# First feed-forward layer by seven products over halves, in units interleaved with the second layer

## The chip, the cores and the metric

The kernel runs on one core of a Trainium2 chip. The metric is the device time of one execution in microseconds (us), the median of several runs. Every run also records the span from its first to its last instruction and the mean clock that the throttle granted TensorE (1.000 is full speed). Runs over 1.5% above the fastest of the same kernel are marked slow and left out of the ratios. Each kernel was timed in rounds with the kernel before on the same chip.

## The reference

Linformer attention over 8 batches of 1024 tokens (8 heads of 64), then a feed-forward pair with a sigmoid-approximated gelu. Only the last two lines matter here.

```python
k_proj = einsum('ks,bhsd->bhkd', E, k);  v_proj = einsum('ks,bhsd->bhkd', F, v)
attn   = softmax(q @ k_proj.T / sqrt(64))          # 64 keys per head
x      = (attn @ v_proj) laid out as 8192 tokens x 512
h      = x @ w_in                                  # 512 -> 2048: the first layer
g      = h * sigmoid(1.702 * h)
out    = g @ w_out                                 # 2048 -> 512: the second layer
```

## The kernel before

The 8192 tokens are worked off in 16 blocks of 512. In each block, TensorE makes the first layer, then the second; scores, softmax sums and values of later blocks are slipped in between as short bursts. The second layer already takes seven products over halves in place of eight (Winograd's variant of Strassen's method): of g, of w_out and of the result each dimension is halved, sums of the halves are made beforehand, and products share banks of PSUM, in which they go on adding.

The first layer in plain form, 16 feature tiles x 4 matmuls of 512 columns, each tile in the next free bank, and read by ScalarE's gelu:

```python
def ffn1(j, fc, ts=slice(0, TB)):
    h_ps = f_tile([P, n])                          # 5 banks in turn
    for kc in range(KC):                           # 4
        nc.tensor.matmul(h_ps, w_in_sb[:, kc, fc*P:(fc+1)*P], xT[j][:, kc, ts], ...)
    nc.scalar.activation(gts[j][:, fc, ts], h_ps, AF.Gelu_apprx_sigmoid)
```

The sums of g for the second layer, on VectorE, made for 4, then 3, then 1 pairs of feature tiles as the gelus come in:

```python
def g_sums(j, c0, n):
    lo, hi = slice(c0, c0+n), slice(FH+c0, FH+c0+n)
    tt(t[0], g[:, lo, THI], g[:, hi, THI], op=ALU.add)       # for product 5
    tt(t[1], t[0], g[:, lo, TLO], op=ALU.subtract)           # for product 6
    tt(t[2], g[:, lo, TLO], g[:, lo, THI], op=ALU.subtract)  # for product 7
    tt(t[3], g[:, hi, TLO], t[1], op=ALU.subtract)           # for product 3
```

The second layer's parts, each of two halves of 8 matmuls with 256 columns. Products 1 and 2 add in one bank, 6, 7 and 4 in a second (which starts as a copy of product 1), 5 and 3 in a third:

```python
def prod(i, tc_, first, final):
    for k in range(FH):                            # 8
        nc.tensor.matmul(gb[bank[i]][:, tc_], a[:, k, tc_*P:(tc_+1)*P], w[:, k], ...)
...
return [p1a, p1b, p5a, p5b, h(6,0), p6b, h(2,0), p2b, h(7,0), p7b, h(4,0), p4b, h(3,0), p3b]
```

The softmax here doesn't subtract the row's maximum and nothing guards it: scores larger than these inputs give would overflow.

Of the kernel before, what the change touches and what calls it, by code (L numbers as in the profile page):

```python
# [17 lines left out]
def kernel(ctx, tc, q, k, v, E, F,  # L18
# [21 lines left out]
    ps_f = ctx.enter_context(tc.tile_pool(name="ps_f", bufs=4, space=PSUM))  # L40
    ps_g = ctx.enter_context(tc.tile_pool(name="ps_g", bufs=1, space=PSUM))
# [4 lines left out]
    ef_f = work.tile([P, JB, DM], F32, name="o_sb")[:, :S // DM].rearrange("p j m -> p (j m)")  # L46
    ef_sb = consts.tile([P, S], BF16, name="ef_sb")
# [84 lines left out]
    opening, f_next, g_next = [True], [0], [0]  # L132

    def f_tile(shape, dt=F32):
        if not opening[0]:
            f_next[0] += 1
            if f_next[0] % 5 == 0:
                return ps_g.tile(shape, dt, name="g3_ps")
        return ps_f.tile(shape, dt, name="f_ps")

    def x_any(shape, dt=F32):
        if not opening[0]:
            return f_tile(shape, dt)
        g_next[0] += 1
        return ps_g.tile(shape, dt, name=f"g{g_next[0] % 4}_ps")
# [18 lines left out]
    ffs = consts.tile([P, J, 2, KP], BF16, name="ffs")  # L164
# [69 lines left out]
    q0s = [[consts.tile([P, 2, 2, P], BF16, name=f"q0T{g}{u}") for u in range(2)] for g in range(2)]  # L234
# [65 lines left out]
    def sums(h):  # L300


        def go():
            d_ps = [x_any([P, TB]), ps_g.tile([P, TB], F32, name="g0_ps")]
            for p in range(HP):
                for e in range(2):
                    r = HI if (p + e) % 2 else LO
                    nc.tensor.matmul(d_ps[e][32 * p:32 * p + 32], ones[r, :32], expT[h][r, p, :], start=True, stop=True)
            den = att.tile([P, 2, TB], F32, name="den", bufs=1)
            for e in range(2):  # L310
                nc.vector.tensor_copy(den[:, e, :], d_ps[e])
            rdens[h] = den
        return go
# [59 lines left out]
    def tok0(p, a):  # L373
# [5 lines left out]
        if p not in xs:  # L379
            xs[p] = work.tile([P, 2, 2, 2, D], BF16, name="x0_sb", bufs=4)  # L380
# [35 lines left out]
    def ffn1(j, fc, ts=slice(0, TB)):  # L416
        if j not in gts:
            gts[j] = work.tile([P, FC, TB], BF16, name="gT", bufs=1)
# [7 lines left out]
    def ffn2(j, n, fcs):  # L426
        b, c = divmod(j, NB2)
        ov = out[b * S:(b + 1) * S, :].rearrange("(p j) m -> p j m", j=J)
        if j not in osb:
            osb[j] = work.tile([P, JB, DM], F32, name="o_sb")  # L430
# [5 lines left out]
        if fcs.stop == FC:  # L436
            nc.scalar.copy(osb[j][:, n, :], o_ps.pop(n))
            if n == JB - 1:
                nc.sync.dma_start(out=ov[:, c * JB:(c + 1) * JB, :], in_=osb[j])
# [7 lines left out]
    tw = consts.tile([P, 4, FH, MH], BF16, name="tw")  # L447
    sg = consts.tile([P, 4, FH, TH], BF16, name="sg")

    def w_sums():  # L450
# [3 lines left out]
        def tt(out_, in0, in1, op=ALU.subtract):  # L454
            def go():
                if not tmp:
                    tmp.append(work.tile([P, JB, DM], F32, name="o_sb").rearrange("p c (d m) -> p (c d) m", m=MH))
# [4 lines left out]
        return [tt(tw[:, 0], b12, b11), tt(None, b22, b12), tt(tw[:, 2], b22, b12), tt(None, None, b11, ALU.add),  # L462
                tt(tw[:, 3], b21, None), lambda: nc.vector.tensor_copy(tw[:, 1], tmp[0])]

    def g_sums(j, c0, n):
# [4 lines left out]
        tt(t[0], g[:, lo, THI], g[:, hi, THI], op=ALU.add)  # L470
        tt(t[1], t[0], g[:, lo, TLO], op=ALU.subtract)  # L471
        tt(t[2], g[:, lo, TLO], g[:, lo, THI], op=ALU.subtract)  # L472
        tt(t[3], g[:, hi, TLO], t[1], op=ALU.subtract)  # L473

    def ffn2_parts(j, last=False):



        b, c = divmod(j, NB2)
        ov = out[b * S:(b + 1) * S, :].rearrange("(p j) m -> p j m", j=J)[:, c * JB:(c + 1) * JB]  # L480
        o = osb[j] = work.tile([P, JB, DM], F32, name="o_sb")
# [5 lines left out]
        bank = {1: 0, 2: 0, 6: 1, 7: 1, 4: 1, 5: 2, 3: 2}  # L487
        gb, u, gl = {}, {}, []

        def prod(i, tc_, first, final):  # L490
            a, w = ops[i]
            for k in range(FH):
                nc.tensor.matmul(gb[bank[i]][:, tc_], a[:, k, tc_ * P:(tc_ + 1) * P], w[:, k],  # L493
                                 start=(first and tc_ == 0 and k == 0), stop=(final and k == FH - 1),
                                 skip_group_check=True)

        def tile_of(n):
            gb[n] = ps_g.tile([P, 2, MH], F32, name=f"g{n}_ps")

        def p1a():  # L500
            tile_of(0)
            prod(1, 0, True, False)

        def p1b():
            prod(1, 1, True, False)
            tile_of(1)
            nc.scalar.copy(gb[1], gb[0])

        def p5a():
            tile_of(2)  # L510
            prod(5, 0, True, False)

        def keep(n):
            u[n] = work.tile([P, 2, MH], F32, name=f"u{n}_sb", bufs=1)
            nc.scalar.copy(u[n], gb[n])  # L515

        def p5b():
            prod(5, 1, True, False)
            keep(2)

        def p6b():
            prod(6, 1, False, False)
            keep(1)

        def put(ts, ms):
            if last:
                nc.sync.dma_start(out=ov[:, ts, ms], in_=o[:, ts, ms])

        def p2b():
            prod(2, 1, False, True)  # L530
            nc.scalar.copy(o[:, 0:2, :MH], gb[0])  # L531
            put(slice(0, 2), slice(0, MH))

        def p7b():
            prod(7, 1, False, False)
            nc.vector.tensor_tensor(o[:, 2:4, MH:], gb[1], u[2], op=ALU.add)  # L536
            put(slice(2, 4), slice(MH, DM))

        def p4b():
            prod(4, 1, False, True)  # L540
            nc.scalar.copy(o[:, 2:4, :MH], gb[1])  # L541
            put(slice(2, 4), slice(0, MH))

        def p3b():
            prod(3, 1, False, True)
            nc.vector.tensor_tensor(o[:, 0:2, MH:], gb[2], u[1], op=ALU.add)
            nc.sync.dma_start(out=ov, in_=o)

        def p3l(tc_):
            def go():  # L550
                for k in range(FH):
                    nc.tensor.matmul(gl[tc_][:, :MH], sg[:, 3, k, tc_ * P:(tc_ + 1) * P], b22[:, k],
                                     start=False, stop=(k == FH - 1), skip_group_check=True)
                nc.vector.tensor_tensor(o[:, tc_, MH:], gl[tc_][:, :MH], u[1][:, tc_], op=ALU.add)
                put(slice(tc_, tc_ + 1), slice(MH, DM))
            return go

        def p5l(tc_):
            def go():
                gl.append(f_tile([P, TB]))  # L560
                for k in range(FH):
                    nc.tensor.matmul(gl[tc_][:, :MH], sg[:, 0, k, tc_ * P:(tc_ + 1) * P], tw[:, 0, k],
                                     start=(k == 0), stop=False, skip_group_check=True)
                if tc_ == 0:
                    u[2] = work.tile([P, 2, MH], F32, name="u2_sb", bufs=1)
                nc.scalar.copy(u[2][:, tc_], gl[tc_][:, :MH])
            return go

        h = lambda i, tc_: lambda: prod(i, tc_, False, False)
        if last:  # L570
            return [p1a, p1b, p5l(0), p5l(1), h(6, 0), p6b, h(2, 0), h(7, 0), p7b, p2b, h(4, 0), p4b, p3l(0), p3l(1)]
        return [p1a, p1b, p5a, p5b, h(6, 0), p6b, h(2, 0), p2b, h(7, 0), p7b,
                h(4, 0), p4b, h(3, 0), p3b]

# [46 lines left out]
    for i, f in enumerate(w_sums()):  # L621
# [19 lines left out]
    at(2, O + 1, scores(4, 0), values(3, 0))  # L641
    at(2, O + 6, scores(4, 1), values(3, 1))
    at(2, O + 9, scores(5, 0), sums(4), gather(4))
    at(2, O + 11, gelu_table)
    at(3, 2, q_dma(3))
    at(3, 3, proj(3), kv_out(3))
    for j in range(3, NBLK - 1):
        at(j, 1, spread(j + 1))
    for b in range(4, B):
        at(NB2 * b - 4, 2, q_dma(b))  # L650
    for j in range(3, NBLK - 1):
        if j + 2 < NBLK:
            at(j, O + 1, scores(j + 2, 1))
        at(j, O + 1, values(j + 1, 0))
        if j + 3 < NBLK:
            at(j, O + 9, scores(j + 3, 0))
        at(j, O + 9, values(j + 1, 1))
        if j + 2 < NBLK:
            at(j, O + 9, sums(j + 2), gather(j + 2))
            at(j, O + 11, gelu_table)  # L660
        if j % NB2 == 0 and j // NB2 + 2 < B:
            at(j, O + 9, proj(j // NB2 + 2), kv_out(j // NB2 + 2))

# [5 lines left out]
    for j in range(NBLK):  # L669
# [15 lines left out]
        if j == 1:  # L685
            opening[0] = False
            g1_ps = ps_g.tile([P, TB], F32, name="g1_ps")
            nc.tensor.matmul(g1_ps, zeros[:, :P], zeros, start=True, stop=True)
        for s, part in enumerate(ffn2_parts(j, j == NBLK - 1)):
            part()  # L690
            filled(j, O + s)
    assert not fill, fill
# [30 lines left out]
```

## Time and profile before

| | kernel before |
|---|---|
| time (three runs; a fourth came with the result) | 491.07 us (490.88 to 491.67) |
| span of the profiled run, granted clock | 489.6 us, 1.000 |
| TensorE, VectorE, ScalarE busy | 98%, 41%, 56% |
| one block without / with a k/v projection | 27.7 / 29.8 us |

The lines themselves stand in the prediction below, with what each column is. An entry in brackets at the end of a timeline line is the time that the engine had idled and what ended it. "PE" are matmuls, "PEld" the weight loads beside them; L numbers are lines of the kernel and differ between the two kernels (first layer: L422 before, L634 after; second layer: L493 before, L552 after).

### The profile page before, as it was taken

The page shows a single profiled execution, that of the slowest core. Times are in us where ns is not written, and L with a number is a line of the kernel's source. Part 1 is how long each engine was busy: PE and PEld are TensorE (multiplying, and loading weights), DVE is VectorE, ACT ScalarE, POOL GpSimd, SP SyncE. Part 2 cuts the span into 40 slices and gives each one's busy share as a digit, 9 for nine tenths or more (in the row PEclk, how much of TensorE's full clock was granted, in tenths as well). Part 3 has the DMA queues.
Part 4 walks back from the last instruction along what each step waited for, and adds up shares of the span by engine and source line. Part 5 has one row for each costly group of instructions (what it writes and reads, how often), then busy time and mean ns, then how long its engine had stood idle before and what let it go on. Part 6 is the DMA issues. An engine that isn't in the chain of part 4 may idle for free.

```text
span 489.6 us, 8708 instructions
## 1 busy us (share of the span) xinstructions
PE 478.1 (98%) x3672; PEld 297.8 (61%) x3707; DVE 202.0 (41%) x435; ACT 275.7 (56%) x445; POOL 83.0 (17%) x103
## 2 busy tenths in 40 slices
PE   8999999999999999999999999999999999999997
PEld 4645458466474755757575674757557474756656
DVE  4514786243542434444233543433453342335241
ACT  2665365465556557564665736575565656555361
POOL 7562251151070070006000240000000000000000
PEclk9999999999999999999999999999999999999999
DMA  9999999999899999699972999356240506032202
GB/s 169 200 189 207 223 160 167 207 212 215 174 94 219 170 183 217 151 172 114 211 143 103 170 113 246 71 171 90 95 87 26 149 1 174 4 124 52 87 0 87
DMA packets 131195, 69.09 MB, mean 141 GB/s; under 512 B 98116, under 2 KB 122708, under 8 KB 129236
## 3 DMA queue, kind: packets, MB, share of 16 engines
q0 software_dynamic: 86816, 30.43, 55.5%
q1 hardware_dynamic: 44260, 37.84, 31.2%
q8 instruction: 29, 0.48, 0.4%
q10 hardware_dynamic: 80, 0.26, 0.2%
q14 instruction: 10, 0.08, 0.1%
HBM read 72.88 MB, written 16.99 MB: 184 GB/s over the span
## 4 chain that ended last, share of the span: by engine, by line
PE 87%; DMA 7%; issue 2%; DVE 2%; ACT 1%; POOL 0%; DVEq 0%; POOLq 0%; ACTq 0%
PE f_ps L422 35%; PE g_ps L493 33%; PE g_ps L422 8%; DMA q_even<-in_q_dram 3%; PE f_ps L434 3%; DMA v_sb<-in_v_dram 3%; PE f_ps L181 2%; PE f_ps L270 2%; DVE o_sb L536 1%; DMA o_sb<-in_E_dram 1%; PE f_ps L189 1%; ACT o_sb L531 1%; ACT expT L289 1%; PE g_ps L150 1%; PE g_ps L270 1%
## 5 line engine op out<-in xcount | busy, mean ns | idle before, releaser
L422 PE MATMUL f_ps<-xT,w_in_sb 128*128 128x512 bf16 (+1 forms) x830 | 190.9, 377 | 1.4
L422 PEld LDWEIGHTS <-w_in_sb 128*128 128x128 bf16 x1032 | 100.6, 98 | 117.0 <-issue 1.2
L424 ACT ACTIVATE gT<-f_ps 128x512 bf16<-128x512 f32 (+1 forms) x214 | 126.9, 593 | 70.0 <-PE f_ps L422 69.0
L493 PEld LDWEIGHTS <-sg 128*128 128x128 bf16 x928 | 89.5, 98 | 16.0 <-DVE sg L473 5.2
L493 PE MATMUL g_ps<-tw,sg 128*128 128x256 bf16 x704 | 82.1, 273 | 0.0
L493 PEld LDWEIGHTS <-gT 128*128 128x128 bf16 x720 | 69.8, 98 | 18.4 <-issue 6.9
L470 DVE TENSOR_TENSOR sg<-gT 128x1024 bf16<-128x1024 bf16 (+2 forms) x45 | 22.9, 510 | 112.1 <-ACT gT L424 112.1
L69 POOL DMA_DIRECT2D q_sb<-in_q_dram x48 | 42.0, 904 | 158.8 <-DMA qT<-q_sb 134.8
L493 PE MATMUL g_ps<-w_out_sb,gT 128*128 128x256 bf16 x480 | 57.6, 273 | 0.0
L422 PE MATMUL g_ps<-xT,w_in_sb 128*128 128x512 bf16 x172 | 44.6, 379 | 0.2
L289 ACT ACTIVATE expT<-f_ps 128x512 bf16<-128x512 f32 (+1 forms) x50 | 26.7, 580 | 16.7 <-PE f_ps L270 13.5
L536 DVE TENSOR_TENSOR o_sb<-g_ps,u_sb 128x512 f32<-128x512 f32 x15 | 10.4, 691 | 62.1 <-PE g_ps L493 37.3
L354 DVE TENSOR_TENSOR xT<-f_ps,rbc 128x512 bf16<-128x512 f32 x40 | 26.2, 684 | 20.3 <-DMA rbc<-rdr 14.1
L424 ACT ACTIVATE gT<-g_ps 128x512 bf16<-128x512 f32 x44 | 26.3, 597 | 12.2 <-PE g_ps L422 11.6
L493 PE MATMUL g_ps<-tw,gT 128*128 128x256 bf16 x240 | 28.7, 272 | 1.5 <-DVE o_sb L536 1.1
L493 PE MATMUL g_ps<-w_out_sb,sg 128*128 128x256 bf16 x224 | 26.7, 273 | 0.0
L541 ACT COPY o_sb<-g_ps 128x512 f32<-128x512 f32 x15 | 8.8, 585 | 31.9 <-PE g_ps L493 31.9
L515 ACT COPY u_sb<-g_ps 128x512 f32<-128x512 f32 x29 | 17.1, 590 | 12.6 <-ACT u_sb L515 8.1
L471 DVE TENSOR_TENSOR sg<-sg,gT 128x1024 bf16<-128x1024 bf16 (+2 forms) x45 | 23.1, 514 | 1.6
L472 DVE TENSOR_TENSOR sg<-gT 128x1024 bf16<-128x1024 bf16 (+2 forms) x45 | 22.8, 507 | 0.0
L473 DVE TENSOR_TENSOR sg<-gT,sg 128x1024 bf16<-128x1024 bf16 (+2 forms) x45 | 22.8, 506 | 0.0
L293 ACT ACT_TABLE_LOAD x15 | 19.2, 1283 | 0.3
(120 smaller groups left out, 343.8 us busy)
## 6 DMA issues: line engine op xcount, KB each, us to landing
out_dram<-o_sb SPq DMA_DIRECT2D x15, 1024.0 KB, 3.9
rbc<-rdr SPq DMA_DIRECT2D x24, 512.0 KB, 5.3
k_sb<-in_k_dram POOLq DMA_DIRECT2D x7, 1024.0 KB, 13.1
v_sb<-in_v_dram POOLq DMA_DIRECT2D x7, 1024.0 KB, 18.1
q_sb<-in_q_dram POOLq DMA_DIRECT2D x48, 128.0 KB, 5.3
w_in_sb<-in_moe_w_in_dram POOLq DMA_DIRECT2D x8, 256.0 KB, 10.6
w_out_sb<-in_moe_w_out_dram POOLq DMA_DIRECT2D x4, 512.0 KB, 12.1
q_even<-in_q_dram POOLq DMA_DIRECT2D x12, 128.0 KB, 15.1
```

The lines of the kernel that those rows point to most:

```text
L69: nc.gpsimd.dma_start(out=qt[b][:, j], in_=qv[:, j])
L289: nc.scalar.activation(expT[h][:, 2 * u + i, ts], s_ps[i], AF.Exp, scale=scale)
L293: nc.scalar.preload_act_table(AF.Gelu_apprx_sigmoid)
L354: nc.vector.tensor_tensor(x_of(h)[:, 2 * u + i, :], n_ps[i], rbc[h][:, 2 * u + i, :], op=ALU.mult)
L422: nc.tensor.matmul(h_ps, w_in_sb[:, kc, fc * P:(fc + 1) * P], xT[j][:, kc, ts], start=(kc == 0), stop=(kc == KC - 1))
L424: nc.scalar.activation(gts[j][:, fc, ts], h_ps, AF.Gelu_apprx_sigmoid)
L470: tt(t[0], g[:, lo, THI], g[:, hi, THI], op=ALU.add)
L471: tt(t[1], t[0], g[:, lo, TLO], op=ALU.subtract)
L472: tt(t[2], g[:, lo, TLO], g[:, lo, THI], op=ALU.subtract)
L473: tt(t[3], g[:, hi, TLO], t[1], op=ALU.subtract)
L493: nc.tensor.matmul(gb[bank[i]][:, tc_], a[:, k, tc_ * P:(tc_ + 1) * P], w[:, k], start=(first and tc_ == 0 and k == 0), stop=(final and k ...
L515: nc.scalar.copy(u[n], gb[n])
```

## The change

From block 3 on the first layer is made by seven products too, which trades 64 matmuls of 512 columns for 112 of 256. Four units n = 0 to 3 each make two pairs of feature tiles. A unit has seven products; "24" below means unit 2, product 4, and "140, 141" are the two halves of the second layer's part 4. Five new jobs come with it: sums of w_in once (block 2), sums of x per block, and per unit a copy of a bank on ScalarE, two copies of banks and two additions on VectorE. Units and second-layer parts are interleaved so that each bank has time to be read. The diff, cut to its core:

```diff
+    def ffn1_unit(j, n):
+        ops = {1: (a11, x[:, KLO, TLO]), 2: (a12, x[:, KHI, TLO]), 3: (late[:, 3], x[:, KHI, THI]),
+               4: (a22, xw[:, 3]), 5: (late[:, 0], xw[:, 0]), 6: (late[:, 1], xw[:, 1]), 7: (late[:, 2], xw[:, 2])}
+        of = {1: 0, 2: 0, 6: 1, 7: 1, 4: 1, 5: 2, 3: 2}     # which products share a bank
+        ...                                                 # 4 matmuls of 256 columns per product
+                if i == 1:
+                    gb[1] = bank(2 + n % 2, [P, 2, TH])
+                    nc.scalar.copy(gb[1], gb[0])
+                elif i == 5:
+                    nc.vector.tensor_copy(u2, gb[2])
+                elif i == 6:
+                    nc.vector.tensor_copy(u1, gb[1])
+                elif i == 7:
+                    add(u2, gb[1], u2)
+                    defer(2, lambda: gelu(g[:, hi, THI], u2))
+                elif i == 2:
+                    gelu(g[:, lo, TLO], gb[0])
+                elif i == 4:
+                    gelu(g[:, hi, TLO], gb[1])
+                elif i == 3:
+                    add(u1, gb[2], u1)
+                    defer(2, lambda: gelu(g[:, lo, THI], u1))
-        o = osb[j] = work.tile([P, JB, DM], F32, name="o_sb")           # two buffers
+                        o[t] = work.tile([P, 2, DM], F32, name=f"o{t}_sb", bufs=1)
+    for j in range(2, NBLK):
+        f(10, 11)
+        if j > 2:
+            g_sums(j, 4, 2, (1,)); units[3][4](); units[3][3]()
+        f(20)
+        burst(j, "a", [1, 2, 4, 3])                # scores and values; the list names the banks
+        f(21)
+        if j > 2:
+            g_sums(j, 6, 2, (1,)); g_sums(j, 4, 4, (2, 3))
+        f(50, 51)
+        burst(j, "b", [0, 1, 2, 4] if j == 2 else [5, 1, 2, 4, 3, 0, 5])  # scores, values, softmax sums, projection
+        f(60, 61)
+        ...
+        go(1, 5)
+        x_sums(j + 1, 1)
+        f(70, 71)
+        if j > 2:
+            g_sums(j, 4, 4, (4,))
+        filled(j, "end")                           # k/v casts of a projection
+        go(6, 2, 11, 140, 141, 7, 15, 16)
+        filled(j + 1, "early")                     # reciprocals and their broadcast
+        go(3, 4, 21, 12, 130, 17)
+        burst(j + 1, "late", [6])                  # transposes of q
+        go(25, 26, 131, 13, 14, 31, 22)
+        g_sums(j + 1, 0, 4)
+        go(27, 35, 36, 32, 23, 24, 37)
```

## The prediction

> **What bounds the kernel now.** I read the page from the top: busy shares, the chain that ended last, the groups; then sums over two neighbouring blocks of 512 tokens (one without, one with a k/v projection), and the timeline around one place where TensorE waits. From the page:
>
> ```profile
> PE 478.1 (98%) x3672; PEld 297.8 (61%) x3707; DVE 202.0 (41%) x435; ACT 275.7 (56%) x445; POOL 83.0 (17%) x103
> PE 87%; DMA 7%; issue 2%; DVE 2%; ACT 1%; POOL 0%; DVEq 0%; POOLq 0%; ACTq 0%
> L422 PE MATMUL f_ps<-xT,w_in_sb 128*128 128x512 bf16 (+1 forms) x830 | 190.9, 377 | 1.4
> L493 PE MATMUL g_ps<-tw,sg 128*128 128x256 bf16 x704 | 82.1, 273 | 0.0
> ```
>
> TensorE is busy for 98% and is 87% of the chain; L422 is the first layer (plain products), L493 the second layer (already seven products over halves). VectorE is at 41%, ScalarE at 56%. The sums of busy time over the two blocks (columns: PE, weight loads, DVE, ACT, POOL, clock, DMA):
>
> ```profile
> 276.04:305.80 29.76, 29.40 (x233) 18.56 (x233) 12.31 (x25) 17.09 (x27) 8.76 (x10) 1.00 1.24 167
> 305.80:333.49 27.69, 27.52 (x216) 17.48 (x217) 10.91 (x22) 17.09 (x27) 0.00 (x0) 1.00 0.57 125
> ```
>
> A plain block takes 27.7 us, one with a projection 29.8 us; TensorE idles for about 0.2 us in each. The timeline of one block, the place where the second layer's part 7 hands its bank to part 4:
>
> ```profile
> 255.83 1.91 PE L493 MATMUL g_ps<-tw,sg 128*128 128x256 bf16 x16
> ...
> 257.83 0.69 DVE L536 TENSOR_TENSOR o_sb<-g_ps,u_sb 128x512 f32<-128x512 f32 x1 [2.46 <-issue]
> ...
> 258.44 0.68 DVE L354 TENSOR_TENSOR xT<-f_ps,rbc 128x512 bf16<-128x512 f32 x1
> 258.58 1.91 PE L493 MATMUL g_ps<-tw,gT 128*128 128x256 bf16 x16
> 259.04 0.68 DVE L354 TENSOR_TENSOR xT<-g_ps,rbc 128x512 bf16<-128x512 f32 x1
> 259.64 0.68 DVE L311 COPY den<-f_ps 128x512 f32<-128x512 f32 x1
> ```
>
> Three rules of this kernel stand in it. A product that goes on adding in a bank waits for the VectorE operation that reads that bank: the read ends at 258.52, the next product starts at 258.58. A reader starts 0.2 to 0.25 us after the product's slot ends. And VectorE operations of 512 fp32 columns follow each other every 0.60 us (0.69 is one of them alone), strictly in program order.
>
> **What the Trainium skill says.** "TensorE: Matmul & The Clock Gate", Back-to-back issue gap: N / 2.4 + 2.5 ns for a warm matmul, so 216 ns at 512 columns and 109 at 256. The trace agrees: 16 wide ones in 3.45 us (216 ns), 16 narrow ones in 1.75 us (109 ns). "VectorE: DVE Perf Modes", the perf-mode tier table: a tensor_tensor with fp32 or PSUM operands gets 1x, with bf16 in SBUF 2x. The trace agrees: 684 ns for 512 columns from PSUM, and 687 ns for 1024 bf16 columns. "PSUM — Partial Sum Buffer", Engine vs sequencer instructions: VectorE and ScalarE queues are strict FIFO. The trace shows nothing overtaking. This page carries my argument: what stands ahead in VectorE's queue delays a bank's release.
>
> **The change, part by part.**
> 1. First layer, blocks 3 to 15: per block 64 matmuls x 0.2158 = 13.81 us become 4 units x 7 products x 4 = 112 matmuls x 0.1094 = 12.25 us. All on the path. Saved: 1.56 us x 13 blocks = **20.2 us**.
> 2. Parts 7 and 4 of the second layer move apart, so the wait shown above (about 0.25 us in a plain block, 0.5 in the last ones) goes: **2 us**. With nothing else the time would be 469 us.
> 3. Added on ScalarE: one bank copy per unit, 4 x 0.58 = 2.3 us per block (17.1 to 19.4 us). It has room.
> 4. Added on VectorE per block: per unit two copies of a bank and two additions, 16 x 0.60 = 9.6 us of slots; four sums of x of 512 bf16 columns at about 0.34 us (between the steps of 0.205 at 256 and 0.47 at 768), 1.4 us. Its 10.9 us busy become about 22 us in a period of some 26: over 80%, and in one stretch more than all.
> 5. In block 2 six sums over 2048 columns for the new weights; the same forms were made for w_out at 1217 ns (twice), 2290 (three times) and 1221: 10.5 us. In the queue with the block's own sums they end some **1.8 us** after product 5 of block 2 needs the last sum.
>
> So I walked the program order of one steady block by hand: a unit product is 0.44 us of TensorE, half a product of the second layer 0.875 us, and VectorE and ScalarE have the spacings above. Time 0 is the first product of unit 0.
> - **The stretch from 8.5 to 16.2 us.** VectorE reads for 03, 17, 25, 26, 131, 13, then the four sums of gT (2.5 us, placed ahead of product 27), then 27, 35, 36. The reads of 17 to 13 end at 13.4. The sums of gT need the gelu of unit 1's sum, which ends at 14.05; they fill the queue to 16.6. Only then comes the addition that reads product 27's bank (done at 17.3). Product 24, which goes on adding in that bank, could start at 15.75 and starts at 17.4; product 37 waits in the same way for the copy after 36 (18.55) and loses 0.8 more. Sum: **2.4 us per block**, 13 blocks: 31 us.
> - **The first product of the next unit 0.** It writes bank 0, which the second sum of the softmax denominators has just used. VectorE must first do two products for xT, two sums of x and the other denominator copy: the copy ends 4.1 us after the burst begins, TensorE is there after 2.6: **1.5 us** in a block without projection, 6 to 7 blocks: 10 us. A projection fills that time.
> - **Blocks with a projection** (4): the k/v casts (0.67 + 0.87 us) delay the copy that product 07 waits for by 0.56 us, and the projection takes over the bank of the first scores of its own burst, whose exponential comes behind a 0.58 us copy: 0.4 more. **4 us**.
> - **Product 5 of the second layer** waits some 0.2 us for the last sums of gT: **2.5 us**.
> Sum of the waits: 31 + 10 + 4 + 2.5 + 1.8 = 49 us. 491 - 22 + 49 = 518 us.
>
> **The rivals.**
> - *The waits hide and the matmuls decide*: 469 to 475 us. For it: VectorE's mean load is only some 80%, the order is clearly laid out with gaps (product 27 and 24 stand 1.75 us apart, against 1.0 us for a read and its latency), and TensorE is the bound today. Against it: those gaps count an empty VectorE queue, and 2.5 us of sums stand in it just there.
> - *A draw*: half of the waits (25 us) eat the gain, 485 to 495 us. For it: my 0.34 us for the sums of x and the hand-over to the gelu are estimates, and one shorter wait moves all after it.
> - *ScalarE becomes the bound*: 19.4 us busy of 26; its table load of 1.28 us and two exponentials stand ahead of a copy that part 7 needs, which gives 0.3 us in blocks where the wait for bank 0 doesn't cover it. Small.
> - *Transfers*: the queue's order changes, but the broadcast of the reciprocals has some 10 us before it is read; I give it nothing.
>
> **Range and chances.** The walk says 518; it has waits only where an order in the program forces them, but a walk by hand tends to count waits that partly cover one another, so I put the time at 512 us. If the matmuls decide after all it is 470 to 478. The range from 478 to 526 leaves most of that out at the bottom and a few us at the top. Chances: faster by over 2% (below 481) 0.20, within 2% 0.17, slower (above 501) 0.63.
>
> **What would show it.** Right: first-layer matmuls of 256 columns every 109 ns; TensorE's busy share falls below 92% although its busy time falls by some 20 us; VectorE's busy time goes from 202 to about 360 us; the list of waits shows matmuls and weight loads waiting for VectorE's unit additions and copies and for the denominator copies, 2 to 4 us per block; a plain block's period rises from 27.7 to 29 to 30 us. Wrong: a period near 26 us with TensorE still at 98%. Then either VectorE gets through its queue faster than one operation per 0.60 us, or the order on its queue is not the program's.

## The result, and the profile after

The kernel after takes 529.34 us (528.01 to 530.66) against 491.37 us (490.88 to 492.49). The ratio is 1.0769, with a 95% interval of 1.0734 to 1.0805: slower by 7.7%. Here and below a ratio is the mean time of one kernel's fast runs over that of the other's of the same rounds, so not quite the ratio of the medians quoted.

The page of the kernel after, busy shares and the chain that ended last:

```profile
PE 474.3 (90%) x4323; PEld 359.4 (68%) x4331; DVE 355.8 (67%) x662; ACT 297.2 (56%) x497; POOL 83.4 (16%) x103
PE 49%; DVE 23%; DMA 18%; ACT 4%; issue 4%; SPq 2%; POOL 1%; DVEq 0%; ACTq 0%; POOLq 0%
```

TensorE's busy share fell from 98 to 90%. VectorE rose from 202 to 356 us busy and is now 23% of the chain, where it had 2%. That TensorE's busy time is only 4 us lower is no count of its work: a row of a narrow matmul is 273 ns long though the next one starts 109 ns later, and some of these matmuls ran at a lower clock.

Sums of busy time from one first product of unit 0 to the next, in three blocks (columns as in the prediction: PE, weight loads, DVE, ACT, POOL, clock, DMA):

```profile
244.64:275.85 31.21, 26.94 (x266) 22.02 (x264) 23.43 (x41) 19.24 (x32) 0.58 (x1) 1.00 0.83 145
275.85:306.95 31.10, 28.71 (x282) 23.27 (x282) 21.89 (x38) 18.15 (x30) 8.59 (x10) 1.00 0.91 134
306.95:339.28 32.33, 28.45 (x266) 22.72 (x263) 23.43 (x41) 19.24 (x32) 0.17 (x1) 0.95 0.75 137
```

The first and third have no projection and took 27.7 us before; the second has one and took 29.8. VectorE, at 22 to 23 us of 31, has time to spare in each, and yet TensorE idles for 2.4 to 4.3 us. The third also has a clock of 0.95.

Who made TensorE wait, from the list of waits (total us, times, longest):

```profile
PE k_ps L634 <- DVE q_even L624: 17.1, 14, 1.3
...
PE k_ps L634 <- DVE q_even L643: 10.2, 17, 0.6
...
PE k_ps L634 <- DVE den L315: 8.7, 7, 1.3
...
PEld L552 <- DVE sg L511: 6.2, 13, 1.1
...
PE k_ps L552 <- DVE sg L511: 1.7, 3, 0.8
```

L624 are the units' additions, L643 the copies after product 6, L315 the denominator copies, L511 the sums of g that product 5 needs: the four of the prediction. The 6.2 us at L511 are a wait of the weight loads, which run ahead; the matmuls themselves waited there for 1.7 us in three places. The stretch that it walked, on the timeline (matmuls and VectorE):

```profile
260.80 0.60 PE L634 MATMUL k_ps<-xT,late 128*128 128x256 bf16 x4
...
261.37 0.69 DVE L517 TENSOR_TENSOR sg<-gT,sg 128x1024 bf16<-128x1024 bf16 x1
...
261.97 0.68 DVE L624 TENSOR_TENSOR q_even<-k_ps,q_even 128x512 f32<-128x512 f32 x1
262.57 0.68 DVE L641 COPY q_even<-k_ps 128x512 f32<-128x512 f32 x1
...
262.71 0.60 PE L634 MATMUL k_ps<-xw,w_in_sb 128*128 128x256 bf16 x4 [1.30 <-DVE q_even L624]
...
263.17 0.68 DVE L643 COPY q_even<-k_ps 128x512 f32<-128x512 f32 x1
...
263.90 0.60 PE L634 MATMUL k_ps<-xw,late 128*128 128x256 bf16 x4 [0.60 <-DVE q_even L643]
```

Product 23 starts at 260.80 and its slot ends at 261.24. Product 24 could follow, but the addition that reads product 27's bank stands behind the four sums of g (the last at 261.37) and ends at 262.65; 24 starts at 262.71. Product 37 waits in the same way for the copy after 36. The slots lost are 1.47 and 0.75 us, a little more than the idle times printed.

Product 5 in two blocks, and the first products of unit 0 at the two ends of a block that has no projection beside it:

```profile
268.98 1.29 DVE L358 TENSOR_TENSOR xT<-k_ps,rbc 128x512 bf16<-128x512 f32 x2 [1.13 <-DMA rbc<-rdr]
...
270.66 1.27 PE L552 MATMUL k_ps<-tw,sg 128*128 128x256 bf16 x10 [0.48 <-DVE sg L511]
...
299.84 2.17 PE L552 MATMUL k_ps<-tw,sg 128*128 128x256 bf16 x16
...
401.00 0.60 PE L634 MATMUL k_ps<-xT,w_in_sb 128*128 128x256 bf16 x4 [1.30 <-DVE den L315]
...
431.05 0.60 PE L634 MATMUL k_ps<-xT,w_in_sb 128*128 128x256 bf16 x4 [1.30 <-DVE den L315]
```

Product 5's 16 matmuls take 2.17 us at 299.84 where such a row without a wait takes 1.91: 0.26 us are lost. Ten of the twelve blocks 3 to 14 show this. The other two lose about 0.6 us; in both, VectorE had just waited 1.1 us for the broadcast of the reciprocals (rbc), as at 268.98. The block from 401.00 to 431.05 takes 30.05 us. Its four waits cost 1.47, 0.75, 0.26 and 1.46 us; without them it would take 26.1 us, against 27.7 before.

One thing the prediction had not: in the chain of the third block, 16 matmuls that elsewhere take 1.75 us follow on these two waits and take 3.40 us, about double:

```profile
326.06 0.60 PE k_ps L634 x4
326.65 3.40 PE k_ps L552 x16
330.06 0.89 PE k_ps L634 x8
```

The same happens behind the same two waits at 139 and 507 us. In the other ten blocks these waits have no such effect.

### The profile page after: what moved, and what is told of

It reads as the page before. It is cut to its first block, busy times and chain, and to the rows that moved or that the text cites. A ratio compares the mean times of both kernels' runs of the same rounds, so it can differ in the third digit from the quotient of the medians.

```text
span 528.2 us, 10499 instructions
## 1 busy us (share of the span) xinstructions
PE 474.3 (90%) x4323; PEld 359.4 (68%) x4331; DVE 355.8 (67%) x662; ACT 297.2 (56%) x497; POOL 83.4 (16%) x103
## 4 chain that ended last, share of the span: by engine, by line
PE 49%; DVE 23%; DMA 18%; ACT 4%; issue 4%; SPq 2%; POOL 1%; DVEq 0%; ACTq 0%; POOLq 0%
PE k_ps L552 25%; PE k_ps L634 19%; DVE xT L358 5%; DMA q_sb<-in_q_dram 4%; DMA rbc<-rdr 3%; DVE sg L511 3%; DMA rdr<-rc 2%; ACT gT L623 2%; DVE sg L517 2%; PE k_ps L274 2%; DMA w_in_sb<-in_moe_w_in_dram 2%; DMA v_sb<-in_v_dram 2%; DMA w_out_sb<-in_moe_w_out_dram 2%; DVE q_even L643 2%; PE k_ps L184 2%
## 5 line engine op out<-in xcount | busy, mean ns | idle before, releaser
L624 DVE TENSOR_TENSOR q_even<-k_ps,q_even 128x512 f32<-128x512 f32 x104 | 70.8, 681 | 60.3 <-PE k_ps L634 59.2
L623 ACT ACTIVATE gT<-q_even 128x512 bf16<-128x512 f32 x104 | 65.5, 630 | 61.2 <-DVE q_even L624 61.2
L634 PEld LDWEIGHTS <-late 128*128 128x128 bf16 x832 | 81.1, 98 | 26.9 <-issue 16.2
L634 PE MATMUL k_ps<-xw,late 128*128 128x256 bf16 x624 | 82.8, 272 | 12.1 <-DVE q_even L643 10.2
L552 PE MATMUL k_ps<-tw,sg 128*128 128x256 bf16 x720 | 88.2, 273 | 3.3 <-DVE sg L511 1.7
L623 ACT ACTIVATE gT<-k_ps 128x512 bf16<-128x512 f32 x104 | 60.2, 591 | 54.4 <-PE k_ps L634 54.4
L552 PE MATMUL k_ps<-w_out_sb,gT 128*128 128x256 bf16 x480 | 64.4, 287 | 0.7 <-ACT k_ps L583 0.7
L634 PE MATMUL k_ps<-xT,w_in_sb 128*128 128x256 bf16 x416 | 56.0, 272 | 7.8 <-DVE den L315 7.8
L634 PE MATMUL k_ps<-xw,w_in_sb 128*128 128x256 bf16 x208 | 31.3, 273 | 16.9 <-DVE q_even L624 16.9
L641 DVE COPY q_even<-k_ps 128x512 f32<-128x512 f32 x52 | 35.5, 684 | 16.0 <-PE k_ps L634 16.0
L426 PE MATMUL k_ps<-xT,w_in_sb 128*128 128x512 bf16 (+1 forms) x195 | 42.6, 370 | 2.0 <-DVE vq L226 1.7
L643 DVE COPY q_even<-k_ps 128x512 f32<-128x512 f32 x52 | 35.5, 683 | 0.4 <-PE k_ps L634 0.2
L634 PE MATMUL k_ps<-xT,late 128*128 128x256 bf16 x208 | 31.2, 273 | 0.0
## 6 DMA issues: line engine op xcount, KB each, us to landing
k_sb<-in_k_dram POOLq DMA_DIRECT2D x7, 1024.0 KB, 11.1
```

What stands on the lines that cost most here:

```text
L426: nc.tensor.matmul(h_ps, w_in_sb[:, kc, fc * P:(fc + 1) * P], xT[j][:, kc, ts], start=(kc == 0), stop=(kc == KC - 1))
L552: nc.tensor.matmul(dst, a[:, k, tc_ * P:(tc_ + 1) * P], w[:, k], start=(first and (one or tc_ == 0) and k == 0), stop=(final and k == FH - 1),
L623: gelu = lambda out_, in_: nc.scalar.activation(out_, in_, AF.Gelu_apprx_sigmoid)
L624: add = lambda out_, in0, in1: nc.vector.tensor_tensor(out_, in0, in1, op=ALU.add)
L634: nc.tensor.matmul(gb[of[i]][:, q], a[:, k, f:f + P], w[:, k], start=(i in (1, 5) and q == 0 and k == 0), stop=(i in (2, 3, 4) and q == 1 ...
L641: nc.vector.tensor_copy(u2, gb[2])
```

## The experiments

Theory: the order on VectorE's queue makes banks come free late, and TensorE waits behind it. Rival one: VectorE simply has too much work, in whatever order. Rival two, which came up on the way: something other than VectorE holds the end once its waits are gone. All twelve kernels gave correct results. The table gives the medians and clocks of the fast runs; e9, e10 and e11 had one slow run each (501.1, 494.7 and 492.5 us), which is left out. The ratio is to the kernel before of the same rounds.

| run | what is different | us | ratio | clock in its runs |
|---|---|---|---|---|
| after | | 529.3 | 1.077 | 0.986 to 0.990 |
| e1 | sums of g behind product 37 | 512.2 | 1.045 | 0.989 to 0.992 |
| e2 | other banks in burst b | 526.0 (520.1 to 527.3) | 1.070 | 0.979 to 0.997 |
| e3 | copy of product 5 on ScalarE | 519.0 | 1.058 | 0.995 to 1.000 |
| e4 | e1 + e2 + sum for product 5 earlier | 503.9 | 1.027 | 0.990 to 0.997 |
| e5 | reordered throughout | 506.9 (501.5 to 507.8) | 1.030 | 0.971 to 0.981 |
| e6 | e5 + copy of product 5 on ScalarE | 507.6 | 1.033 | 0.970 to 0.983 |
| e7 | after, zeros in one wait | 527.5 (525.1 to 532.5) | 1.075 | 0.993 to 1.000 |
| e8 | e4 + transposes of q later | 509.4 | 1.035 | 0.986 to 0.987 |
| e9 | e5 + two output buffers | 493.8 (492.5 to 496.5) | 1.004 | 0.988 to 0.997 |
| e10 | e9 + broadcast earlier | 486.6 (485.1 to 487.7) | 0.991 | 0.996 to 1.000 |
| e11 | e10 + block 2 mended | 487.6 (483.5 to 488.8) | 0.990 | 0.993 to 1.000 |
| e12 | e10 with the sums of g back in front | 508.4 | 1.038 | 0.995 to 1.000 |

### e1: the sums of g behind product 37

```diff
-        g_sums(j + 1, 0, 4)
         go(27, 35, 36, 32, 23, 24, 37)
+        g_sums(j + 1, 0, 4)
```

> The four sums of gT (2.5 us on VectorE) are placed behind product 37 instead of ahead of product 27; the work is the same. Theory (order of VectorE's queue): the waits of 1.30 us before product 24 and 0.60 us before product 37 go in all 13 blocks (25 us), and with them the stretches at half clock (about 5 us); the sums then delay the last sum for product 5 by 0.5 to 1 us in 12 blocks. Expected 500 to 510 us. Rival (VectorE has too much work, in whatever order): the waits only move, 522 us or more.

Measured 512.2 us, 17 us less with the same work; the rival wanted 522 or more. It is 2 us above the theory's range. In its trace the waits before 24 and 37 are gone; the wait for product 5's last sum grew, since those sums now stand in front of it, from 0.48 to 1.43 us in the block shown and from 1.7 us in 3 places to 8.3 us in 7 over the run. Late broadcasts have a part in that: VectorE waited 4.9 us for them, 2.2 in the kernel after. The clock stayed at 0.99, against the theory: three stretches at half clock now stand behind other waits (2.38 us for product 5's sum, 1.70 and 1.35 us for an output copy). From the timeline of e1:

```profile
269.28 1.26 PE L552 MATMUL k_ps<-tw,sg 128*128 128x256 bf16 x10 [1.43 <-DVE sg L511]
```

### e2: other banks for the softmax sums

```diff
-[5, 1, 2, 4, 3, 0, 5]
+[5, 0, 2, 4, 3, 1, 5]
```

> Only bank numbers change: the second denominator sum goes to bank 1 instead of bank 0, the second score tile to bank 0. Theory: the first product of unit 0 no longer waits 1.30 us for the denominator copy in the 7 blocks without projection that show it; 9 us less, 519 to 522 us. Rival (VectorE is late by amount, and the wait comes back at the next bank it owns): 526 us or more.

The wait for the denominator copies is gone from the list, and the other two are as they were (17.6 and 10.2 us), so the wait did not come back elsewhere. The median is nevertheless 526.0, the rival's number. The single runs suggest why: 520.1 us at a clock of 0.997, 525.5 at 0.987, 526.5 at 0.979 and 527.3 at 0.980. (1 - clock) x time is an estimate of the time lost to the clock, if TensorE is busy while it is low: 1.6, 6.8, 11.1 and 10.5 us, and the times less these are 518.5, 518.7, 515.5 and 516.8. By this sum, most of the 9 us gained were lost to the clock in three of four runs. The kernel after lost 5.3 us in this way (0.010 x 528), which agrees with its trace: three stretches that take 1.65 us too long each, 5.0 us in all.

### e3: less work on VectorE, same order

```diff
-                    nc.vector.tensor_copy(u2, gb[2])
+                    nc.scalar.copy(u2, gb[2])
```

> The copy of product 5's bank goes from VectorE to ScalarE, order untouched: 52 operations, 31 us of VectorE slots less, 30 us of ScalarE more. Theory (order): the sums of gT still stand ahead of product 27's read and still wait for the same gelu, so only one read of 0.6 us ahead of them goes; the wait before product 24 falls by at most 0.6 us and the one before 37 by up to 0.6 us: 513 to 522 us. Rival (amount of VectorE work): most of the loss goes, 497 to 505 us.

Measured 519.0 us, in the theory's range and far from the rival's. Of 31 us of VectorE work taken away, 10 came back. Before product 24 the same 1.30 us are waited (16.9 us in all), because what stands ahead is the same; before 37 the wait fell from 10.2 to 2.4 us in all. With it the clock rose to 1.000 in three runs of four.

### e4: three orders together

```diff
+        if j > 2:
+            g_sums(j, 6, 2, (1,))
         burst(j, "a", [1, 2, 4, 3])
         f(21)
         if j > 2:
-            g_sums(j, 6, 2, (1,))
             g_sums(j, 4, 4, (2, 3))
```

This stands beside the edits of e1 and e2.

> Sums behind product 37, bank swap, and the last sum for product 5 ahead of the softmax burst, together. Theory: 1.9 us x 13, 1.3 us x 7, 0.4 us x 12 and 5 us of half clock go: about 44 us less, 484 to 494 us, so within 2% of the kernel before. Rival (amount): 515 us or more.

Measured 503.9 us: neither. The waits of before are gone, and a new one has come, in the list of waits of e4:

```profile
PE k_ps L274 <- ACT o_sb L590: 13.8, 11, 3.8
...
ACT o_sb L590 <- DMA out_dram<-o_sb: 5.7, 6, 3.0
```

The scores (L274) wait for bank 0, which ScalarE copies to the output tile (L590) late: part of the time it waits until the block before has been written to memory, for the change gave that tile one buffer. My bank swap had put scores on bank 0, so this was in part my own doing.

### e8: the transposes of q behind part 3's output

```diff
-        go(3, 4, 21, 12, 130, 17)
-        burst(j + 1, "late", [6])
-        go(25, 26, 131, 13, 14, 31, 22)
+        go(3, 4, 21, 12, 130, 17)
+        go(25, 26, 131)
+        burst(j + 1, "late", [6])
+        go(13, 14, 31, 22)
```

> The three orders run with one more move: the transposes of q (7.3 us on the queue that also issues the outputs) are issued behind part 3's output instead of ahead of it. That run came out at 504 instead of 484 to 494 us, and its trace shows TensorE waiting 13.8 us for the copy of part 2, which itself waits for the output of the block before. Theory (output issued late behind the transposes): those 14 us go, 488 to 494 us. Rival (copy late because of ScalarE's own queue, table load and exponentials ahead of it): 500 us or more.

509.4 us, 5 us worse than e4: this theory fell. The wait of the scores grew to 19.4 us. The output still stands behind the broadcast on the same queue, and VectorE waited 10.8 us for broadcasts, 2.6 in e4. Perhaps the transposes, issued later, now fall into the time in which the next broadcast is needed; no run separates this.

### e5 and e6: reordered throughout, without and with the copy on ScalarE

```diff
# shortened: the cases for block 2 and the last blocks are left out
-        f(20); burst(j, "a", [1, 2, 4, 3]); f(21)
-        g_sums(j, 6, 2, (1,)); g_sums(j, 4, 4, (2, 3))
+        f(20, 21); g_sums(j, 6, 2, (1,))
+        burst(j, "a", [1, 3, 4, 2])
+        g_sums(j, 4, 4, (2, 3))
-        burst(j, "b", [5, 1, 2, 4, 3, 0, 5])
+        burst(j, "b", [5, 0, 4, 2, 1, 3, 4])
-            g_sums(j, 4, 4, (4,))
+            g_sums(j, 0, 8, (4,))
-        g_sums(j + 1, 0, 4)                        # ahead of product 27
+        g_sums(j + 1, 0, 4, (1, 2, 3))             # behind product 37
# and: gelu table load moved from "b" to "end", k/v casts from "end" ahead of unit 0, the edit of e8; e6: the edit of e3 as well
```

> Best version by the theory, all of it order and bank numbers: sums of gT behind product 37 and the fourth sum in one piece, both halves of part 2 and the last sum for product 5 ahead of the softmax burst, banks of the bursts such that none is asked for before its reader is through, k/v casts ahead of the next unit 0, gelu table load behind the bank copies, and the transposes of q issued behind the output of part 3. Theory: nearly all waits go, 470 to 480 us. Rival (VectorE, at over 80% of the remaining period, can't keep up in any order): 490 us or more.

> The version before with the copy of product 5's bank on ScalarE as well. Theory: if VectorE's queue holds up the last few products, another 2 to 5 us go; if ScalarE is then late (its busy share is near 80%), it is 2 to 6 us slower than without. 468 to 482 us. Rival (amount): well below the version without, by 10 us or more.

506.9 and 507.6 us: both ranges missed, and e6 shows that the amount of VectorE's work is not what is left. VectorE's own waits on TensorE's path are nearly gone. What holds now, in e5's list of waits:

```profile
ACT o_sb L590 <- DMA out_dram<-o_sb: 17.2, 4, 4.6
...
DVE xT L358 <- DMA rbc<-rdr: 11.0, 4, 3.0
```

So rival two becomes the likely one from here on: the single output buffer, and the broadcast of the reciprocals (rbc). e9 and e10 test it. The clock fell to 0.971 in the profiled run, 14.7 us by the sum of e2.

### e9 and e10: two output buffers, then the broadcast earlier

```diff
-    o[t] = work.tile([P, 2, DM], F32, name=f"o{t}_sb", bufs=1)
+    o[t] = work.tile([P, 2, DM], F32, name=f"o{t}_sb", bufs=2 - t)
# room: k_b with one buffer in place of two, x_sb with two in place of four
# e10 as well:
-        go(6, 2, 11, 140, 141, 7, 15, 16)
-        filled(j + 1, "early")
+        go(6, 2, 11, 140, 141)
+        filled(j + 1, "early")
+        go(7, 15, 16)
```

> The reordered version with two buffers for the first output tile instead of one (room made by one buffer less for two small tiles). The reordered version came out at 507, not 470 to 480 us; its trace has the copy of part 2 waiting 17.2 us for the output of the block before, whose write stands on the queue behind the broadcast of the reciprocals; TensorE waits behind that, and the clock falls to 0.971. Theory (new wait: a single output buffer): the wait for the output goes and with it most of the half clock: 480 to 492 us; what is left is the late broadcast (11 us waited on VectorE). Rival (the broadcast alone holds everything): 500 us or more.

> The same with the reciprocal and its broadcast issued about 1.3 us of products earlier, ahead of unit 0's product 7. Theory (single output buffer and late broadcast were the two waits left): 474 to 484 us. Rival (broadcast is late because the loads of q, k and v crowd it, so earlier issue gains nothing): same as the run before.

493.8 us for e9: 13 us came with the second buffer, 2 us less than the range had it; the wait for the output is gone from its list, and that for the broadcast is what is left. e10 took it from 493.8 to 486.6 us, 3 us short of its range. It is the first version that beats the kernel before, by less than the 2% that would count as faster: ratio 0.991, interval 0.987 to 0.994. Two windows of e10:

```profile
205.00:235.00 30.00, 29.73 (x295) 24.42 (x294) 24.87 (x45) 19.03 (x32) 8.74 (x10) 1.00 0.98 144
235.00:265.00 30.00, 30.00 (x299) 25.41 (x297) 24.44 (x42) 20.45 (x35) 0.00 (x0) 1.00 0.74 144
```

In the second TensorE is busy all the time, beside a VectorE at 81%. That share is no bound then; the order is.

### e12: the one line undone in the best order

```diff
+        g_sums(j + 1, 0, 4, (1, 2, 3))
         go(27, 35, 36, 32, 23, 24, 37)
-        g_sums(j + 1, 0, 4, (1, 2, 3))
```

> The early-spread version with one thing undone: the sums of gT again ahead of product 27. Theory (order of VectorE's queue is the main cost): the waits of 1.3 and 0.6 us before products 24 and 37 come back in 13 blocks and with them some half clock: 20 to 32 us more, 507 to 519 us. Rival (they were only the waits in front; others would have hidden them): 497 us or less.

508.4 us, 22 us more than e10 and 21 more than e11, which ran in the same rounds; this is in the theory's range. The two waits are back, in the timeline of e12:

```profile
255.62 0.60 PE L634 MATMUL k_ps<-xw,w_in_sb 128*128 128x256 bf16 x4 [0.70 <-DVE q_even L624]
256.82 0.60 PE L634 MATMUL k_ps<-xw,late 128*128 128x256 bf16 x4 [0.60 <-DVE q_even L643]
```

They are 1.30 us in this block, where they are 1.90 in the kernel after, since here the fourth sum of g is elsewhere. Counted as lost slots (the idle times plus about 0.16 us each for getting going again, as read above), 1.62 us x 13 blocks are 21 us. The clock stayed at 0.995 to 1.000. This is the cleanest measure of the queue's order: same work, one line moved.

### e7: zeros in the wait

```diff
+        w_ps = bank(0, [P, TB])
+        for _ in range(10):
+            nc.tensor.matmul(w_ps[:, :TH], zeros[:, :P], zeros[:, :TH], start=True, stop=True)
         go(24, 37)
```

> The changed kernel with ten matmuls of zeros (1.1 us) in a free bank ahead of product 24, in the wait of 1.30 us; nothing else. Theory (idle TensorE costs clock besides its own length): mean granted clock 1.000 instead of 0.99, and 3 to 6 us less, 523 to 527 us, though no wait is shorter. Rival (clock falls for another reason, the load or the chip): clock 0.99 and 528 to 532 us.

The clock rose from 0.986 to 0.990 in the kernel after to 0.993 to 1.000, as the theory has it, and its trace has none of the three stretches at half clock. The median, 527.5 us, is only 2 us lower, between the two ranges, and the four runs spread from 525.1 to 532.5. So idling costs clock here; how much time filling it gains this run does not settle.

### e11: block 2 mended

Its edit puts the k/v casts of block 2 ahead of the reciprocals that wait for a gather, and the first two sums of w_in in block 1.

> The early-spread version with block 2 mended: the k/v casts ahead of the reciprocals that wait for a gather (TensorE waited 1.72 us for them), and the first two weight sums (2.4 us of VectorE) in block 1. Theory: 2 to 4 us less than 487, 482 to 486 us, so 1 to 2% faster than the kernel before. Rival (block 2 waits for k, v and q loads in any case): 486 to 489 us.

487.6 us (483.5 to 488.8 in the fast runs): no gain over e10. The trace shows 1.3 us gained by the first unit (114.5 in place of 115.8 us), and TensorE waiting 7.3 us behind late broadcasts of later blocks, where e10 had 2.6. So the gain was probably given back to transfers.

## Why the prediction was right or wrong

**Direction and mechanism: right.** Products over halves ran at the 109 ns per matmul predicted, VectorE's busy time came to 356 us (360 were predicted), and the four waits appear at nearly the sizes walked. Two of its signs came less clearly: TensorE's busy time fell by 4 us and not 20, for the reason given with the page, and a plain block took 30.05 us (29 to 30 were predicted) or, behind a block with a projection, 31.2. One reading was a slip without weight: by its own lines the block with a projection idles 0.36 us, not 0.2. The rival that the matmuls would decide is refuted for this order. Another order comes closer to it: e10 has TensorE at 96%, but at 486.6 us is still 12 us above the 475 us of that rival.

**The size: wrong.** 529 us lie above the range of 478 to 526, and the time given was 512. The terms, in the profiled runs (489.6 to 528.2 us of span; measured terms are lost TensorE slots read from the timelines times blocks, so all are estimates):

| term of the sum | predicted us | measured us |
|---|---|---|
| matmuls and parts 7 and 4 | -22 | -20 (1.6 x 13, from the plain block above) |
| products 24 and 37 | 31 | 2.2 x 13 = 29 |
| first product of unit 0 | 10 | 1.4 x 7 = 10 |
| blocks with a projection | 4 | 3 to 4 |
| product 5 of the second layer | 2.5 | 0.26 x 10 + 0.6 x 2 = 4 |
| up to part 6 of block 2 | 1.8 | 4.6 (115.9 us after, 111.3 before) |
| last block's own parts | none | 1.6 |
| half clock | none | 3 x 1.65 = 5 |
| sum | 27 | 38 |

The spans differ by 38.6 us.

- **The step that failed is the one in "Range and chances"**: "a walk by hand tends to count waits that partly cover one another, so I put the time at 512 us", with 526 as the top. The walk said 518, and the waits didn't cover one another: the terms that it had for waits in the blocks add up to 46 to 47 us as measured, against 47.5 predicted. What lay outside the walk then came on top.
- **A term was missing: the clock**, 5 us. I read 1.00 in every window of the kernel before and took it as given, but its blocks had no waits of this length. Windows at 0.95 and the doubled matmuls are in the profile after, and e7 ties the clock to the idling. The kept traces go further: inside the blocks, each of their 24 stretches at half clock (in after, e1, e2, e4, e5, e6, e8 and e9) begins in a wait of TensorE or within about 1 us behind one. Not every wait does it: 1.30 us without the 0.60 behind it in 13 blocks of e3, 0.70 and 0.60 us in 13 blocks of e12, and one wait of 3.03 us in e12 did not.
- **The two ends were too small**: up to part 6 of block 2 the walk had 1.8 us and 4.6 were lost. 1.0 of these are product 5's wait, 0.9 a wait of part 2; 2.6 stand there already when block 2's second layer begins. These 2.6 stay unexplained; runs with the same code up to there differ by up to 1.8 us at this point. The last block's own parts (1.6 us) were not counted.
- **The transfers, given nothing, cost little in the kernel after** (the two late broadcasts above, some 0.7 us) and became the bound once VectorE's waits were gone (e5, e9, e10). I had put 470 to 480 us on e5 and was wrong there by the same kind of omission: a wait counted only where it was already seen.
- **Why the change as given is slower**, then: a gain of 20 us is outweighed by some 58 us of new losses. The largest, 29 us at products 24 and 37, comes from a single call: the sums of g, 2.5 us of work, placed ahead of the short reads that free banks. Moving it back gained 17 us (e1); moving three of the four sums forward again cost 21 to 22 us (e12).

What stays open: which length and spacing of idling makes the clock fall (it did after waits of 1.30 and 0.60 us in 3 of 13 blocks, and not in the others), and how far the remaining variation of e10 and e11 (483 to 489 us in the fast runs) is transfers and how far clock.

## What to carry to other kernels

When a change fills a second engine to 80%, its mean share says little: walk the order of its queue against every bank that the first engine waits for, and keep long work that nothing waits for soon (here 2.5 us of sums) behind the short reads that free banks. Add such waits up rather than discount them, and allow for a loss of clock if TensorE idles for 1 to 2 us at a time (here 5 us of 528). After the first waits are removed expect the next, so check what single-buffered outputs and broadcasts on a shared queue can take before promising the full gain.

## What the Trainium skill lacked or had wrong

- "TensorE: Matmul & The Clock Gate", Why this matters for your kernels, advises no idle gaps above about 3 us to keep the clock. In the kernel after it fell to half for 16 matmuls (3.40 us in place of 1.75) after two waits of 1.30 and 0.60 us with four matmuls between them. The three such stretches cost 5 us in all. The page gives no length or spacing of shorter gaps that do it.
- "VectorE: DVE Perf Modes", The TRN2 errata: the row PSUM to SBUF, 120 + columns cycles at 0.96 GHz, gives an estimate of 658 ns for 512 fp32 columns. The traces show 684 ns for one operation, and 0.60 us from one to the next when they follow each other. For queues it is this spacing that counts, and the page doesn't give it for PSUM.
